# FNet mixing and top-1 expert layer on one core: row sums taken with the residual add, four one-hot tables on ScalarE, and the handover between the two stages re-ordered

## Chip, core and metric

One core of a Trainium2 chip runs the whole kernel. The metric is device time in microseconds (us); the number compared is the median of several runs. The engines are TensorE (PE; its weight loads are listed as PEld), VectorE (DVE), ScalarE (ACT), GpSimd (POOL) and SyncE (SP, which here only issues DMAs). Each runs its own instructions in order and waits for the others by semaphores.

## What is computed

The input is 2048 tokens of 512 values. The first half mixes them with a Fourier transform, the second sends each token to one of eight experts:

```python
x = A_x
h = x + Real(DFT_seq(DFT_hidden(layernorm(x))))      # by DFT matrices that are inputs
n = layernorm(h)
logits = n @ w_gate                                   # 8 experts
e = argmax(logits)                                    # top 1; its softmax over one value
out = h + gate * (silu(n @ w1[e]) @ w2[e])            # w1: 512 x 1376, w2: 1376 x 512
```

## The kernel before

**First half.** Tokens are folded by symmetry into 4 groups and 8 result blocks of 2 x 128 tokens; `second(i)` is the last product of block i (12 matmuls of 512 columns into one PSUM bank, `bank(i)`). `sums_of(i)` then adds the bank to the input rows (two row sets of 128 tokens: `direct` and `turned_row`, the latter as two instructions, 510 + 2 columns) and takes mean and variance of the two row sets. It has two ways: `far_stats`, two passes on ScalarE (a sum, then a square with that sum as bias, L247 and L248), for three of four row sets, and `own_stats` on VectorE (`bn_stats`, `bn_aggr`, L254 to L257) for the rest. `settle(c)` makes 1/deviation and -mean/deviation for four row sets (a square root on ScalarE, L264, six small VectorE instructions, L270 to L276) and stores the 512 values and these two numbers of each token to `rows` in DRAM (`leave`, L586, on SP). The last group (c = 3: row sets 12 to 15, "late") is not waited for in DRAM: its rows go straight from SBUF.

**Routing.** `gate(i)` makes the logits (small matmuls woven between those of `second`), `route` (L593 to L602, VectorE) picks the experts, `rank_them` (PE) and `take_ranks` (VectorE) number the tokens of each expert. `place(t)` writes a 128 x 304 one-hot table of row set t (`lanes == rank`, L640): t = 0 to 3 on GpSimd, the rest on VectorE. 16 matmuls (L849, "turned", into c2b) multiply them by `mine`, which holds token numbers and logits, so that each expert gets a list of its tokens. ScalarE copies the list (L850 `up`), PE turns it (L852), ScalarE copies it into `table` (L855).

**Handover.** Expert 0 comes first and takes up to 232 early tokens, gathered from `rows` by two indirect DMAs on GpSimd's queue (L865, into `hold`), plus up to 72 late ones. Ahead of the gathers stands a tiny read, `peek` (L857). The late ones: `spot(t)` (L647) makes 72-column one-hots for row sets 12 to 15, `normal_late` (L870) and L878 normalise these rows (`late`), and `late_rows` (L652) multiplies the two, 16 matmuls into c2a with a filler matmul behind each. `stand` (L887) turns the gathered rows (`xn`), `upright0` splits the turned rows into high and low parts (`t0h`, `t0l`). `split` is the helper for this everywhere: a cast on ScalarE (L117), a subtraction on VectorE (L118). `prep(b)` does the same to a weight block b ("pair"), `load(b)` fetches it. `fill(n)` issues n matmuls of ones by zeros, 512 columns, of which nobody uses the result (L376).

**Second half.** 8 experts x 11 steps (`first`: 12 matmuls into hp, silu twice on ScalarE, a subtraction on VectorE; `then`: 12 matmuls into yp). Beside it `recheck` compares the DFT matrices with the symmetries that the first half assumes (L700, VectorE, 32 pairs of 512 KB blocks and four more); `AT_ONCE` pairs are read and checked in the first half, one half pair per step in the second half.

**What sets the order.** PE, VectorE, ScalarE and SP run their instructions in the order in which the code stands; a line that stands later can't pass one that waits.

Of the kernel before, what the change touches and what calls it, by code (L numbers as in the profile page):

```python
# [8 lines left out]
F32 = mybir.dt.float32  # L9
# [31 lines left out]
AT_ONCE = 5  # L41
# [18 lines left out]
def fnet_moe(ctx: ExitStack, tc: tile.TileContext, xq, wrep, wline, wcol0, dmat, xturn, dturn, wcol, wchk, dchk, wsm, xres, wgen, dgen, wexp, out):  # L60
# [43 lines left out]
    peek = const.tile([NL, 8], F32, name="peek")  # L104
# [36 lines left out]

    def prep(b):
        if b in raws:
            ready[b] = halves()
            split(*ready[b], raws.pop(b))
# [15 lines left out]
    with ExitStack() as pa:  # L161
# [99 lines left out]
        def deviations(pool, n, mv):  # L261

            sd = pool.tile([P, n], F32, name=f"sd{n}")
            nc.scalar.activation(sd, mv[:, :, 1], AF.Sqrt, bias=eps)  # L264
            return sd

        def roots(pool, n, sd, mv, nm, to=None):
# [3 lines left out]
            nc.vector.tensor_scalar(v, mv[:, :, 1], EPS, -0.5, op0=ALU.add, op1=ALU.mult)  # L271
# [4 lines left out]
            nc.vector.scalar_tensor_tensor(nm_to, nm, 1.0 / ROOT, r_to, op0=ALU.mult, op1=ALU.mult)  # L276
# [210 lines left out]
        spots = stood.tile([P, NS - NL, LATE], F32, name="spots")  # L487
        ours = stood.tile([P, NS - NL], F32, name="ours")
# [79 lines left out]
        def direct(i):  # L568
            c, j = divmod(i, 2)
            x = X[c][:, 2 * j, :D]  # L570
            nc.vector.tensor_add(x, bank(i), x)
            return x

        def turned_row(i):
            c, j = divmod(i, 2)
            x, y = X[c][:, 2 * j + 1, :D], bank(i)
            two = x.rearrange("p (a c) -> p a c", a=2)
            nc.vector.tensor_add(two[:, :, 1:], ap(y, HALF + 1, [[-HALF, 2], [1, HALF - 1]]), two[:, :, 1:])
            nc.vector.tensor_add(x[:, 0::HALF], y[:, 0::HALF], x[:, 0::HALF])
            if i == 2 * SPEC:  # L580
                nc.scalar.copy(x[0:1, :], alone[0])
            return x
# [43 lines left out]
        def cards():  # L626

            nc.vector.tensor_sub(card[:, :, 1], tops, tops)
            for i in range(2):
                nc.vector.tensor_tensor(  # L630
                    mine[:, :, i, :], chosen, card[:, :, i:i + 1].bitcast(F32).to_broadcast([P, NS, E]), op=ALU.mult)

        def place(t, eng=None):
# [6 lines left out]
            (eng or nc.vector).tensor_scalar(places[t], lanes[:, :CAPS[0]], rank[:, t:t + 1], None, op0=ALU.is_equal)  # L640
# [3 lines left out]

        def spot(t):
            i = t - NL
            nc.vector.tensor_scalar(  # L647
                spots[:, i, :], lanes[:, EARLY:EARLY + LATE], rank[:, t:t + 1], ours[:, i:i + 1], op0=ALU.is_equal, op1=ALU.mult)
# [8 lines left out]
        w2 = {}  # L657
        gates = C[1][0][:, :TC].rearrange("p (i e) -> p i e", i=NS // 2)
        mvs, nms = {}, {}
        FAR_H = (0, 1, 2)  # L660
        POOLS = 4

        def sums_of(i):
# [4 lines left out]
            for q, fold in ((2 * j, direct), (2 * j + 1, turned_row)):  # L668
                x = {q: fold(i)}
                if q in FAR_H and (c, q) != (NCH - 1, 1):  # L670
                    far_stats(work, x, (q,), mvs[c], nms[c])
                else:
                    own_stats(work, x, (q,), mvs[c], nms[c])

        def settle(c, a=0, b=4):

            mv, nm = mvs[c][:, a:b, :], nms[c][:, a:b]
            roots(work, b - a, deviations(work, b - a, mv), mv, nm, (X[c][:, a:b, D], X[c][:, a:b, D + 1]))
            leave(c, a, b)
# [142 lines left out]
        check(2)  # L822
        load(0)
        load(1)
        load(2)
        run(second(3), several(gate(4), gate(5), gate(6), gate(7)), 4)
        lone_gate(*alone[1:])
        route()
        run(second(4))
        got = rank_them()  # L830
        sums_of(3)
        sums_of(4)
        run(second(5))
        take_ranks(*got)
        cards()
        for t in range(POOLS):
            place(t, nc.gpsimd)
        for t in range(POOLS, 10):
            place(t)
        sums_of(5)  # L840
        run(second(6))
        settle(1)
        settle(2)
        for t in range(10, NS):
            place(t)
# [8 lines left out]
        whole = table.rearrange("p q a e -> p (q a e)")  # L854
# [13 lines left out]
        def normal_late(t):  # L868
            x = X[3][:, t - NL, :]
            nc.scalar.activation(held[t], x[:, :D], AF.Identity, scale=x[:, D:D + 1], bias=x[:, D + 1:])  # L870

        sums_of(6)
        nc.vector.tensor_scalar(ours, whom[:, NL:], float(E), None, op0=ALU.is_equal)
        for t in range(NL, NS):
            spot(t)
        sums_of(7)
        settle(3)
        for t in range(NL, NS - 1):  # L878
            normal_late(t)
        x = X[3][:, 3, :]  # L880
        nc.vector.tensor_scalar(held[NS - 1], x[:, :D], x[:, D:D + 1], x[:, D + 1:], op0=ALU.mult, op1=ALU.add)
# [11 lines left out]
        for t in range(NL, NS):  # L893
            late_rows(upr[2], t)
        prep(0)
        prep(1)
        softmax(work, table[:, :, 1, :])
# [626 lines left out]
```

## Time and profile before

| | us |
|---|---|
| median of 3 runs | 434.7 (433.95 to 434.83) |
| the profiled execution | 432.62 |
| its span, first to last instruction | 430.9 |
| busy: PE, DVE, ACT, POOL | 403.3, 346.3, 251.0, 70.3 |

The profile is one execution. Its time lies 1.72 us above its span (launch and end) and 2.1 us below the median of the runs. Busy time says how much of the span an engine had work. A busy PE isn't PE at full rate: its clock has two levels here, 2.4 GHz (granted clock 1.00) and 1.2 GHz (0.50), and a matmul at the lower one shows up as busy for longer. The second half starts at 139.22 us, with the first matmul into hp.

### The profile page before, as it was taken

The numbers are of one execution on the slowest core, as the hardware profiler recorded it, in microseconds if no ns is written. First come the engines' busy times: TensorE is split into PE (matmuls) and PEld (weight loads), VectorE is DVE, ScalarE is ACT, GpSimd is POOL, SyncE is SP. The second block draws the span as 40 slices with busy tenths as digits, with TensorE's granted clock in tenths as the row PEclk, the third lists the DMA queues.
The fourth block names the chain that finished last, engine by engine and source line by source line (L and its number), as shares of the span: only waits on it lengthen the run. The fifth ranks groups of instructions, "written<-read, shape, count | busy, mean of one in ns | idle before, by whom it ended". The sixth has DMA issues, their size and how long they took to land. (4 is left out here: it accounts for less than half of the span.)

```text
span 430.9 us, 7840 instructions
## 1 busy us (share of the span) xinstructions
PE 403.3 (94%) x2769; PEld 358.7 (83%) x2769; DVE 346.3 (80%) x752; ACT 251.0 (58%) x482; POOL 70.3 (16%) x69
## 2 busy tenths in 40 slices
PE   5699999999778999999999999999999999899992
PEld 2489998878446999999999999998888888799981
DVE  3689975788964765698999899999999999866641
ACT  5989721614366565647556564665765665666640
POOL 1000000000320220332044023404304102300101
PEclk9699999999859999999999999999999999999998
DMA  8973453382166389669899989999999999754201
GB/s 295 412 270 120 175 199 115 137 288 94 68 213 205 108 310 363 202 232 376 326 322 370 343 300 346 378 358 355 366 348 376 400 372 386 232 192 163 86 0 53
DMA packets 32385, 110.43 MB, mean 256 GB/s; under 512 B 4113, under 2 KB 4113, under 8 KB 31698
## 3 DMA queue, kind: packets, MB, share of 16 engines
q1 hardware_dynamic: 29298, 100.77, 64.7%
q0 software_dynamic: 3040, 9.08, 5.9%
q8 instruction: 23, 0.38, 0.3%
q14 instruction: 24, 0.20, 0.1%
HBM read 101.44 MB, written 8.60 MB: 255 GB/s over the span
## 5 line engine op out<-in xcount | busy, mean ns | idle before, releaser
L117 ACT CAST pair<-far 128x1024 fp32r<-128x1024 f32 x77 | 80.7, 1049 | 55.3 <-PE yp L159 55.3
L118 DVE TENSOR_TENSOR pair<-far,pair 128x1024 fp32r<-128x1024 f32 x77 | 93.9, 1219 | 23.2 <-ACT pair L117 23.0
L157 PE MATMUL hp<-th,pair 128*128 128x256 f32 (+3 forms) x308 | 89.9, 292 | 2.4 <-DVE pair L118 2.4
L700 DVE CUSTOM_DVE_ANT_0 scrap<-raw 128x256 bf16<-128x256 f32 (+3 forms) x106 | 88.3, 833 | 1.9 <-DMA raw<-in_wchk 0.4
L158 PE MATMUL hp<-tl,pair 128*128 128x256 f32 (+3 forms) x308 | 87.6, 284 | 0.7 <-DVE tl L118 0.6
L159 PE MATMUL hp<-th,pair 128*128 128x256 f32 (+3 forms) x308 | 87.5, 284 | 0.0
L157 PEld LDWEIGHTS hp<-th,pair 128*128 128x128 f32 x308 | 58.0, 188 | 8.4 <-DVE pair L118 7.1
L992 ACT ACTIVATE sl<-hp 128x256 f32<-128x256 f32 (+4 forms) x88 | 34.5, 392 | 46.7 <-PE hp L159 45.1
L158 PEld LDWEIGHTS hp<-tl,pair 128*128 128x128 f32 x308 | 58.0, 188 | 2.3 <-DVE tl L118 1.3
L159 PEld LDWEIGHTS hp<-th,pair 128*128 128x128 f32 x308 | 58.0, 188 | 0.0
L157 PE MATMUL yp<-hh,pair 128*128 128x304 f32 (+3 forms) x176 | 53.0, 301 | 0.2 <-DVE yT L1024 0.2
L158 PE MATMUL yp<-hl,pair 128*128 128x304 f32 (+3 forms) x176 | 51.2, 291 | 0.0
L159 PE MATMUL yp<-hh,pair 128*128 128x304 f32 (+3 forms) x176 | 51.2, 291 | 0.0
L1040 POOL DMA_INDIRECT out_h<-o,ids x20 | 36.8, 1842 | 87.6 <-DVE o L1039 87.1
L996 DVE TENSOR_TENSOR hl<-sl,hh 128x256 fp32r<-128x256 f32 (+4 forms) x88 | 38.0, 432 | 6.2 <-ACT hh L995 3.5
L945 POOL DMA_INDIRECT hg<-rows,src x17 | 21.1, 1241 | 133.9 <-issue 49.2
L157 PE MATMUL yp<-pair,hl 128*128 128x512 f32 x88 | 35.6, 405 | 0.0
L158 PE MATMUL yp<-pair,hh 128*128 128x512 f32 x88 | 34.7, 395 | 0.0
L159 PE MATMUL yp<-pair,hh 128*128 128x512 f32 x88 | 34.6, 393 | 0.0
L995 ACT ACTIVATE hh<-hp 128x256 fp32r<-128x256 f32 (+4 forms) x88 | 34.1, 388 | 0.0
L157 PEld LDWEIGHTS yp<-hh,pair 128*128 128x128 f32 x176 | 33.1, 188 | 0.8 <-DVE yT L1024 0.4
L158 PEld LDWEIGHTS yp<-hl,pair 128*128 128x128 f32 x176 | 33.1, 188 | 0.0
(418 smaller groups left out, 803.8 us busy)
## 6 DMA issues: line engine op xcount, KB each, us to landing
far<-in_wexp SPq DMA_DIRECT2D x77, 512.0 KB, 7.2
raw<-in_wchk SPq DMA_DIRECT2D x64, 512.0 KB, 5.8
raw<-in_wexp SPq DMA_DIRECT2D x11, 512.0 KB, 5.4
rows<-x SPq DMA_DIRECT2D x4, 1028.0 KB, 6.1
raw<-in_wrep SPq DMA_DIRECT2D x8, 512.0 KB, 7.2
xt<-in_xturn SPq DMA_DIRECT2D x4, 1024.0 KB, 8.5
x<-in_xq SPq DMA_DIRECT2D x3, 1024.0 KB, 8.5
raw<-in_dchk SPq DMA_DIRECT2D x4, 512.0 KB, 5.3
```

Of the source, the lines that this page charges most:

```text
L117: nc.scalar.copy(hi, src)
L118: (eng or nc.vector).tensor_sub(lo, src, hi.bitcast(F32))
L157: nc.tensor.matmul(ps, sl, mh, start=first, stop=False)
L158: nc.tensor.matmul(ps, sh, ml, start=False, stop=False)
L159: nc.tensor.matmul(ps, sh, mh, start=False, stop=last)
L700: nc.vector.tensor_tensor_reduce(left, a, b, scale, 0.0, op, ALU.max, to)
L945: nc.gpsimd.indirect_dma_start(out=got[:n, i, :], out_offset=None, in_=rows, in_offset=bass.IndirectOffsetOnAxis(ap=src[:n, i:i + 1], axis=0))
L992: nc.scalar.activation(sl, ps, AF.Silu)
L995: nc.scalar.activation(hh, ps, AF.Silu)
L996: nc.vector.tensor_sub(hl, sl, hh.bitcast(F32))
L1040: d = nc.gpsimd.indirect_dma_start(out=out, out_offset=bass.IndirectOffsetOnAxis(ap=ids[:n, i:i + 1], axis=0), in_=o[:n], in_offset=None, ...
```

## The change

- `direct` and `turned_row` add by scalar_tensor_tensor with an accumulator, so that the sum over the row comes out of the add; for `turned_row` two partial sums are added by one more small instruction (L695 of the new code). ScalarE then takes one pass per row set (`spread`, a square with the sum as bias) instead of two, and `bn_stats`/`bn_aggr` are gone. One row set (of block 2, whose row 0 is replaced after the add) keeps a second ScalarE pass (`whole_sum`). `roots` and `deviations` take other constants for the other scale.
- `place`: row sets 4, 6, 8, 10 on ScalarE, each as two activations (Abs, then Relu of 1 - |x|); none on GpSimd. `cards` (which makes `mine`) goes from VectorE to GpSimd.
- `spot` and its tables are gone: `late_rows` uses columns 232 to 303 of the tables from `place`, and the factor that keeps only expert 0's tokens goes into the scale and bias of the late rows. One filler stands among the four products of a row set instead of four.
- Order: gates 6 and 7 run beside `second(4)` instead of `second(3)`, `sums_of(3)` ahead of `route`; `settle(1)` (and its store) ahead of `take_ranks`; `settle(2)` after three one-hots; the matmuls of "turned" run beside 8 fillers, and 22 fillers instead of 8 stand behind them, 6 instead of 3 ahead of hp, none around `stand`. The casts of the first two weight blocks (`high`) run ahead of `route`, four blocks are prepared ahead of hp instead of three. `peek` is gone. The exp of the gates, with its two table loads, goes into expert 0's second step; the rows of expert 1 are normalised after the silu of step 6 instead of before.
- `AT_ONCE` 4: one pair of `recheck` goes from the first half to the second.

VectorE, from the numbering of the tokens to the adds of the last group. Before (`x_123` is the third group's input, `fh`, `fl` are one-hot tables; some tables are GpSimd's and don't stand here):

```order
L624 SCALAR_TENSOR_TENSOR rank<-chosen,past,rank 128x4
L628 TENSOR_TENSOR card<-tops 128x16
L630 TENSOR_TENSOR mine<-chosen,card 128x16x8 x2
L640 TENSOR_SCALAR fh_1201<-lanes,rank 128x304 x2
L640 TENSOR_SCALAR fl_1204<-lanes,rank 128x304 x2
L640 TENSOR_SCALAR fh_1207<-lanes,rank 128x304 x2
L571 TENSOR_TENSOR x_123<-c0a,x_123 128x512
L578 TENSOR_TENSOR x_123<-c0a,x_123 128x2x255
L579 TENSOR_TENSOR x_123<-c0a,x_123 128x2
L254 BN_STATS st<-x_123 128x6
L255 BN_AGGR mv_1161<-st 128x2
L257 TENSOR_SCALAR nm_1162<-mv_1161 128x1
```

After (`x_124` is now the third group's input; the piece from the same instruction on):

```order
L633 SCALAR_TENSOR_TENSOR rank<-chosen,past,rank 128x4
L579 SCALAR_TENSOR_TENSOR x_124,nm_1195<-c3b,x_124 128x512
L586 SCALAR_TENSOR_TENSOR x_124,part<-c3b,x_124 128x2x255
L588 SCALAR_TENSOR_TENSOR x_124,part<-c3b,x_124 128x2
L695 TENSOR_TENSOR nm_1195<-part 128x1
L579 SCALAR_TENSOR_TENSOR x_124,nm_1195<-c0a,x_124 128x512
L586 SCALAR_TENSOR_TENSOR x_124,part<-c0a,x_124 128x2x255
L588 SCALAR_TENSOR_TENSOR x_124,part<-c0a,x_124 128x2
L695 TENSOR_TENSOR nm_1195<-part 128x1
L654 TENSOR_SCALAR fh_1214<-lanes,rank 128x304 x2
L654 TENSOR_SCALAR fl_1217<-lanes,rank 128x304
```

Both adds of the third group now stand ahead of every one-hot, each with its sum; the statistics on VectorE are gone.

ScalarE, from the table of tokens to the split of the turned rows. Before:

```order
L855 COPY table<-c1a 128x48
L247 ACTIVATE junk,nm_1313<-x_124 128x512
L248 ACTIVATE junk,mv_1312<-x_124,nm_1313 128x512
L247 ACTIVATE junk,nm_1313<-x_124 128x512
L248 ACTIVATE junk,mv_1312<-x_124,nm_1313 128x512
L264 ACTIVATE sd_1339<-mv_1312,eps 128x4
L870 ACTIVATE late<-x_124 128x512 x3
L117 CAST pair<-raw 128x1024 x2
L151 ACT_TABLE_LOAD
L151 ACTIVATE ex<-table 128x24
L899 ACT_TABLE_LOAD
L899 ACTIVATE warm<-eps 128x1
```

After:

```order
L891 COPY table<-c1a 128x48
L679 ACTIVATE junk,mv_1338<-x_125,nm_1339 128x512 x4
L273 ACTIVATE sd_1358<-mv_1338,eps 128x4
L905 ACT_TABLE_LOAD
L905 ACTIVATE warm<-eps 128x1
L919 ACTIVATE late<-x_125,ours 128x512 x3
L118 CAST t0h<-c2a 128x4x72
L118 CAST t0h<-c0a 128x4x128
L118 CAST t0h<-c3a 128x4x104
L145 CAST pair<-raw 128x1024 x2
```

The late group's statistics are still four passes, one per row set now; one table load stands ahead of `late`, and the casts of weights, the exp and the gathered rows' normalisation no longer stand between `late` and the split.

PE, the 16 matmuls that make the list of tokens ("turned", into c2b). Before (`fh_1195` and `fl_1198` are GpSimd's tables):

```order
L849 MATMUL c2b<-fh_1201,mine 16x304 x2
L849 MATMUL c2b<-fl_1204,mine 16x304 x2
L849 MATMUL c2b<-fh_1207,mine 16x304 x2
L849 MATMUL c2b<-fl_1256,mine 16x304 x2
L849 MATMUL c2b<-fh_1259,mine 16x304 x2
L849 MATMUL c2b<-fl_1262,mine 16x304 x2
L849 MATMUL c2b<-fh_1195,mine 16x304 x2
L849 MATMUL c2b<-fl_1198,mine 16x304 x2
L852 MATMUL c1a<-identr,up 128x16 x3
```

After, its last part (`fh_1244`, `fl_1249`, `fh_1254` and `fl_1259` are here the tables that ScalarE writes, row sets 4, 6, 8 and 10):

```order
L884 MATMUL c2b<-fh_1244,mine 16x304
L886 LDWEIGHTS ones
L886 MATMUL c2a<-zero,ones 128x512
L884 MATMUL c2b<-fl_1249,mine 16x304
L884 MATMUL c2b<-fh_1254,mine 16x304
L886 LDWEIGHTS ones
L886 MATMUL c2a<-zero,ones 128x512
L884 MATMUL c2b<-fl_1259,mine 16x304
L884 MATMUL c2b<-fh_1264,mine 16x304
L886 LDWEIGHTS ones
L886 MATMUL c2a<-zero,ones 128x512
L884 MATMUL c2b<-fl_1267,mine 16x304 x2
```

A filler now follows each second product, and GpSimd's four tables, last before, are replaced by ScalarE's, which stand three places from the end.

The diff, cut to its core:

```diff
-AT_ONCE = 5
+AT_ONCE = 4
...
-        def direct(i):
+        def direct(i, to):
...
-            nc.vector.tensor_add(x, bank(i), x)
+            nc.vector.scalar_tensor_tensor(x, bank(i), 1.0, x, op0=ALU.mult, op1=ALU.add, accum_out=to)
...
-        def place(t, eng=None):
+        def place(t, far=False):
...
-            (eng or nc.vector).tensor_scalar(places[t], lanes[:, :CAPS[0]], rank[:, t:t + 1], None, op0=ALU.is_equal)
+            if far:
+                gap = work.tile([P, CAPS[0]], F32, name="gap", bufs=2)
+                nc.scalar.activation(gap, lanes[:, :CAPS[0]], AF.Abs, scale=-1.0, bias=rank[:, t:t + 1])
+                nc.scalar.activation(places[t], gap, AF.Relu, scale=-1.0, bias=one)
+            else:
+                nc.vector.tensor_scalar(places[t], lanes[:, :CAPS[0]], rank[:, t:t + 1], None, op0=ALU.is_equal)
...
+        def spread(x, total, to):
+            junk = work.tile([P, D], BF16, name="junk", bufs=1)
+            nc.scalar.activation(junk, x, AF.Square, bias=total, scale=-float(D), accum_out=to)
...
+            x = direct(i, total[:, a:a + 1])
+            y = turned_row(i, part[:, 0:1], part[:, 1:2])
+            spread(x, total[:, a:a + 1], mv[:, a, 1:2])
+            if i == 2 * SPEC:
+                whole_sum(y, total[:, b:b + 1])
+            else:
+                nc.vector.tensor_add(total[:, b:b + 1], part[:, 0:1], part[:, 1:2])
+            spread(y, total[:, b:b + 1], mv[:, b, 1:2])
...
-        for t in (*range(POOLS, NS), *range(POOLS)):
-            nc.tensor.matmul(turned, flat(t), places[t], start=t == POOLS, stop=t == POOLS - 1)
+        order_t = [t for t in range(NS) if t not in FAR_T]
+        order_t[-3:-3] = FAR_T
+        for n, t in enumerate(order_t):
+            nc.tensor.matmul(turned, flat(t), places[t], start=n == 0, stop=n == NS - 1)
+            if n % 2:
+                nc.tensor.matmul(C[2][0], ones, zero, start=True, stop=True)
...
-                    spots[:, t - NL, :], start=t == NL and k == 0, stop=t == NS - 1 and k == KD - 1)
-                fill(1, 2, True)
+                    places[t].bitcast(F32)[:, EARLY:], start=t == NL + 1 and k == 0, stop=t == NS - 1 and k == KD - 1)
+                if k == 1:
+                    fill(1, 2, True)
...
-        fill(8, 2, True)
-        nc.gpsimd.dma_start(peek, rows.rearrange("(t p) d -> t p d", p=P)[:NL, 0, :8])
+        fill(FILL1, 2, True)
...
+                if (r, j) == (0, 1):
+                    softmax(work, table[:, :, 1, :])
+                    warm = work.tile([P, 1], F32, name="warm", bufs=1)
+                    nc.scalar.activation(warm, eps, AF.Silu)
```

## Rows read from the trace of the kernel before

**Rows 1.** Busy us by stretch: PE, PEld, DVE, ACT, POOL; clock, DMA share, GB/s.

```profile
117.00:121.00 4.00, 3.51 (x14) 1.79 (x14) 3.86 (x13) 0.45 (x2) 0.00 (x0) 0.50 1.03 366
...
300.00:350.00 50.00, 49.06 (x309) 42.25 (x309) 49.62 (x97) 31.99 (x61) 10.41 (x6) 1.00 1.00 374
```

**Rows 2.** PE's timeline, routing to second half: start, us, what, [idle before <-releaser].

```profile
100.65 0.16 PE L566 MATMUL c1a<-g,ah 1*1 1x8 f32 x1
...
112.72 0.44 PE L849 MATMUL c2b<-fh,mine 128*16 128x304 f32 x2
...
113.27 0.44 PE L849 MATMUL c2b<-fh,mine 128*16 128x304 f32 x2
116.73 0.72 PE L849 MATMUL c2b<-fl,mine 128*16 128x304 f32 x2 [3.02 <-DVE fl L640]
...
118.91 0.71 PE L849 MATMUL c2b<-fl,mine 128*16 128x304 f32 x2
...
120.84 3.59 PE L376 MATMUL c2b<-zero,ones 128*128 128x512 bf16 x8
126.45 0.70 PE L652 MATMUL c2a<-spots,late 128*128 128x72 f32 x2 [2.02 <-ACT late L870]
...
133.79 0.38 PE L376 MATMUL c2b<-zero,ones 128*128 128x512 bf16 x1
134.00 0.34 PE L652 MATMUL c2a<-spots,late 128*128 128x72 f32 x2
134.18 1.24 PE L376 MATMUL c2b<-zero,ones 128*128 128x512 bf16 x5
135.54 0.66 PE L887 MATMUL c0a<-ident,xn 128*128 128x128 f32 x4
136.03 1.03 PE L376 MATMUL c2b<-zero,ones 128*128 128x512 bf16 x4
...
139.22 1.38 PE L987 MATMUL hp<-t0h,pair 128*128 128x304 f32 x8
```

**Rows 3.** VectorE's timeline in the same stretch.

```profile
103.13 0.17 DVE L602 TENSOR_REDUCE early<-chosen 128x1 bf16<-128x12 bf16 x1
...
117.45 0.66 DVE L640 TENSOR_SCALAR fl<-lanes,rank 128x304 fp32r<-128x304 f32 x2
118.03 0.68 DVE L571 TENSOR_TENSOR x<-c0b,x 128x512 f32<-128x512 f32 x1
...
124.58 0.18 DVE L270 RECIPROCAL r<-sd 128x4 f32<-128x4 f32 x1 [0.56 <-ACT sd L264]
```

**Rows 4.** ScalarE's timeline in the same stretch.

```profile
121.80 0.72 ACT L248 ACTIVATE junk<-x,nm 128x512 bf16<-128x512 f32 x1
...
122.65 0.63 ACT L247 ACTIVATE junk<-x 128x512 bf16<-128x512 f32 x1
...
125.59 2.22 ACT L870 ACTIVATE late<-x 128x512 f32<-128x512 f32 x3 [1.04 <-DVE x L276]
...
129.71 1.28 ACT L151 ACT_TABLE_LOAD   x1
131.01 0.22 ACT L151 ACTIVATE ex<-table 128x24 f32<-128x24 f32 x1
```

**Rows 5.** The page's group of the check's passes.

```profile
L700 DVE CUSTOM_DVE_ANT_0 scrap<-raw 128x256 bf16<-128x256 f32 (+3 forms) x106 | 88.3, 833 | 1.9 <-DMA raw<-in_wchk 0.4
```

**Rows 6.** Line L700, its accumulator reads: ns min/median/max, first and last start.

```profile
L700 DVE DVE_READ_ACCUMULATOR2_ANT off<- x108: 70/82/88, 72.0 to 371.5; 128x1 f32 x108
```

**Rows 7.** VectorE's timeline in the second half: an add by scalar_tensor_tensor.

```profile
299.85 0.74 DVE L1039 SCALAR_TENSOR_TENSOR o<-tp,usel,hg 128x512 f32<-128x512 f32 x1
```

**Rows 8.** Waits from 300 to 380 us: total, times, longest.

```profile
PEld hp L157 <- DVE pair L118: 6.5, 14, 1.3
```

**Rows 9.** DMA issues: KB each, median us from issue to landing.

```profile
rows<-x SPq DMA_DIRECT2D x4, 1028.0 KB, 6.1
...
hold<-rows,src POOLq DMA_INDIRECT x5, 4.4
```

More of the change, by code (lines that the diff above doesn't have):

```diff
@@ L140, in halves, with high, low @@
         return both[:, 0, :], both[:, 1, :]
+    def high(b):
+        ready[b] = halves()
+        nc.scalar.copy(ready[b][0], raws[b])
+    def low(b):
+        hi, lo = ready[b]
+        nc.vector.tensor_sub(lo, raws.pop(b), hi.bitcast(F32))
     def prep(b):
         if b in raws:
-            ready[b] = halves()
-            split(*ready[b], raws.pop(b))
+            high(b)
+            low(b)
     def softmax(pool, z):
@@ L667, in sums_of, with settle @@
                 mvs[c], nms[c] = fresh_stats(work, 4)
[L668 to L678, printed above, removed]
+            mv, total = mvs[c], nms[c]
+            part = work.tile([P, 2], F32, name="part")
+            a, b = 2 * j, 2 * j + 1
+            x = direct(i, total[:, a:a + 1])
[6 more added lines that the diff above has]
+            spread(y, total[:, b:b + 1], mv[:, b, 1:2])
+        def settle(c, a=0, b=4, between=None):
+            mv, total = mvs[c][:, a:b, :], nms[c][:, a:b]
+            unit = float(D) ** -3
+            sd = deviations(work, b - a, mv, unit)
+            if between:
+                between()
+            roots(work, b - a, sd, mv, total, (X[c][:, a:b, D], X[c][:, a:b, D + 1]), unit, -1.0 / D)
             leave(c, a, b)
@@ L821, in fnet_moe @@
         sums_of(2)
[L822 to L826, printed above, removed]
+        for b in range(4):
+            load(b)
+        run(second(3), several(gate(4), gate(5)), 2)
+        sums_of(3)
+        fourth = second(4)
+        last_gates = several(gate(6), gate(7))
+        for _ in range(2):
+            next(fourth)
+            for _ in range(KD):
+                next(last_gates)
         lone_gate(*alone[1:])
+        high(0)
+        high(1)
         route()
-        run(second(4))
+        run(fourth)
         got = rank_them()
-        sums_of(3)
+        settle(1)
+        cards()
+        take_ranks(*got)
+        run(second(5))
         sums_of(4)
[L833 to L838, printed above, removed]
+        sums_of(5)
+        for t in range(3):
             place(t)
-        sums_of(5)
+        settle(2)
         run(second(6))
[L842 to L845, printed above, removed]
+        mixed = [(t, t in FAR_T) for t in range(3, NS)]
+        for t, far in mixed:
+            place(t, far)
         run(second(7))
         turned, standing = C[2][1][:2 * E, :CAPS[0]], C[1][0]
-        for t in (*range(POOLS, NS), *range(POOLS)):
-            nc.tensor.matmul(turned, flat(t), places[t], start=t == POOLS, stop=t == POOLS - 1)
+        whole = table.rearrange("p q a e -> p (q a e)")
+        order_t = [t for t in range(NS) if t not in FAR_T]
[4 more added lines that the diff above has]
+                nc.tensor.matmul(C[2][0], ones, zero, start=True, stop=True)
         nc.scalar.copy(upright[:, :CAPS[0]], turned)
@@ L891, in upright0 @@
             split(T0[0][:, :, lo:lo + n], T0[1][:, :, lo:lo + n], ps)
-        for t in range(NL, NS):
+        for t in (NL + 1, NL, *range(NL + 2, NS)):
             late_rows(upr[2], t)
-        prep(0)
-        prep(1)
-        softmax(work, table[:, :, 1, :])
-        warm = work.tile([P, 1], F32, name="warm", bufs=1)
-        nc.scalar.activation(warm, eps, AF.Silu)
-        upright0(2, EARLY, LATE)
+        low(0)
         with nc.allow_low_precision(reason="counts up to 18"):
@@ L911, in fnet_moe @@
             x = xg0[:n, i, :]
-            if i:
-                nc.vector.tensor_scalar(xn0[:n, i, :], x[:, :D], x[:, D:D + 1], x[:, D + 1:], op0=ALU.mult, op1=ALU.add)
-            else:
-                nc.scalar.activation(xn0[:n, i, :], x[:, :D], AF.Identity, scale=x[:, D:D + 1], bias=x[:, D + 1:])
-            fill(4, 2, True)
-            stand(i)
+            nc.vector.tensor_scalar(xn0[:n, i, :], x[:, :D], x[:, D:D + 1], x[:, D + 1:], op0=ALU.mult, op1=ALU.add)
+        stand(0)
+        stand(1)
+        upright0(2, EARLY, LATE)
+        for i, n in front:
             upright0(i, i * P, n)
+        low(1)
         prep(2)
-        fill(3, 2, True)
+        load(6)
+        prep(3)
+        fill(6, 2, True)
     with ExitStack() as pb:
```

75 lines of the change are left out of this document (37 added, 38 removed).

## The prediction, as it went on record

> **What bounds the kernel now.** I read busy time by stretch first. From 139 us on PE is busy nearly throughout, so whatever moves the first hp matmul (139.22 [rows 2]) moves the end, as long as the second half keeps its length. Ahead of it PE's timeline names two waits: 3.02 us for VectorE's one-hots, up to 116.73, and 2.02 us for ScalarE's late rows [rows 2]. Behind the first the granted clock is 0.50, its lower level, in 117 to 121 [rows 1]. What comes behind runs at the lower clock: eight fillers take 3.59 us [rows 2], 0.45 each, against 0.21 later (133.79 to 134.00 [rows 2]); the 16 late products with their fillers take 126.45 to 134.18 [rows 2], 7.7 us. From there to hp are another 5.0 us. So the stretch from 113 to 139 is a chain VectorE, PE, ScalarE, VectorE, ScalarE, PE, in which each engine waits for one other, and half of it is PE at half clock.
>
> **The list of tokens.** The last gate matmul ends at 100.81, VectorE's route at 103.30 [rows 2, 3], 2.5 us behind it; PE fills this with `second(4)` and doesn't wait. Now half of that block (6 matmuls of 512 columns, at the filler's 0.21 [rows 2] 1.3 us) stands ahead of the last gates: route starts 1.3 us later, half a block is left to cover its 2.5 us, and PE waits about 1.1. So the numbering, and all of PE behind it, come 1.0 us later; the first product of "turned" starts at 113.7 instead of 112.72 [rows 2]. These take 0.14 each at the full clock (two pairs in 0.55, 112.72 to 113.27 [rows 2]), 16 of them 2.2, and the eight new fillers 1.7: the end is at 117.6 if PE never waits, against 119.62 now (118.91 and 0.71 [rows 2]).
>
> Does VectorE keep up? No row shows an add that gives its sum. The plain add takes 0.68 [rows 3], scalar_tensor_tensor on the same shape 0.74 [rows 7], an accumulator read 0.08 [rows 6]; nearest to it is 0.74 and 0.08, of which some 0.08 overlaps with the next instruction (two adds start 0.60 apart for 0.68 long ones). I take 0.75, with 0.66 (the read is free) and 1.48 (twice the plain 0.74) as ends. With the two-column add, its read and the sum of the parts a call of `sums_of` is then 1.95 us, no shorter than now on average: it saves ScalarE's passes, not VectorE's time. Behind route (104.6 now) VectorE has: `settle` 1.0 (124.58 to 125.59, where ScalarE's `late` gets its rows [rows 3, 4]), the ranks 1.3, two `sums_of` 3.9, three one-hots at 0.29 (two in 0.58, 117.45 to 118.03 [rows 3]) 0.9, `settle` 1.0, nine one-hots 2.6, with 0.4 of waits 115.7. PE wants the last at 117.3: 1.6 us of cover. ScalarE's four tables are eight passes of 304 columns, at most half of a 512-column pass (0.72 [rows 4]) plus a fixed part, 2.5 to 3 us from 112: done by 115, wanted at 116.5. The order shows no table load among them. GpSimd's `mine` has from 104.6 to 113.7. PE waits no more in this step, so the clock stays up.
>
> **Late group.** The way from the list's end to the fillers (1.2 us, 119.62 to 120.84 [rows 2]) has three small matmuls at full clock now, 0.3 less: ScalarE is free 2.2 earlier. It has four passes before the root, as before, but all of the longer kind: 0.85 from start to start (121.80 to 122.65 [rows 4]) against 0.76, +0.2. So `settle(3)` starts 2.0 earlier, at 122.6, and ends at 123.6. VectorE has its last sums at 119.6 (115.7 and 3.9) and the fourth pass starts at 121.4: cover 1.8. Then: the factors 0.2, row set 13 on VectorE 0.7, first late product 124.5. ScalarE's table load starts at 122.6, takes 1.28 [rows 4], hides behind `settle`'s small instructions and is over at 124.1 with its dummy; three late rows at 0.74 (2.22 for three [rows 4]) are ready at 124.8, 125.6, 126.3. A row set on PE is four products at 0.18 (134.00 to 134.18 [rows 2]) and one filler, 0.93: end at 128.2, against 134.18. The 22 fillers (4.6 us from 118.6) end at 123.2, so PE waits 1.3 us in front.
>
> The Trainium skill (ScalarE: Activation LUTs, What ACT_TABLE_LOAD costs) gives 2.66 us for a switch of tables, drain included; here the next activation starts 1.30 after the load [rows 4]. By the page three late rows would come 1.3 later, and hp with them.
>
> **To hp.** Gathered rows: the third group's store is issued at 113.1, with the median 6.1 us [rows 9] down at 119.2, about when the list is there; the gathers land 4.4 later [rows 9], at 123.7 and 125.1. Without `peek` nothing else stands ahead of them. VectorE wants them at 126.4 (behind `low(0)` 1.15 and the counts 0.75) and is done at 127.6, before PE is free. Then eight transposes (four in 0.49, 135.54 to 136.03 [rows 2]) 1.0, and six fillers 1.3, behind which the last cast (0.5) hides: hp at 130.5, against 139.22. **Gain 8.7 us.** If the gathers landed later, each us behind 126.4 would cost one.
>
> **Second half.** (a) One more pair of the check: 88.3 us [rows 5] for 34 pairs (32, and the four blocks counted as two) is 2.6 us of VectorE. From 300 to 350 it is busy for 49.62 of 50 [rows 1], and PE's weight loads wait for its pairs 14 times, 6.5 us up to 380 [rows 8]: there VectorE sets the pace. But each step has one half pair anyway; the added one lengthens the check by two steps at its end, into steps where VectorE has room. Between 0 and 2.6 I take 1.2. (b) Two table loads and the exp in expert 0's second step, 3.0 us of ScalarE. Four blocks lie ready instead of three and the step after needs no new one; ends 0 and 3.0, I take 0.3, since silu is wanted only two steps later. (c) Loads: the fifth block waits for `low(1)` and is issued 1 us behind hp; it has some 10 us. Nothing.
>
> **Sum:** -8.7 + 1.2 + 0.3 = -7.2. On the profiled execution 432.6 gives 425.4; it ran 2.1 below the median, so 434.7 gives **427.5**.
>
> **Rivals.**
> 1. *The clock falls all the same*, in the 1.3 us ahead of the late rows. Against it: before, it fell behind a wait of 3.02, more than twice as long. For it: the margins above add up, a chain 1.5 us longer makes that wait twice as long. Price: 16 products and four fillers at half clock, 3.7 more. 431.2.
> 2. *The second half gives it back*: the whole 2.6 for the pair and 3.0 for the loads, 4.1 more than taken. For it: VectorE's 49.62 of 50. 431.6.
> 3. *Half rate for the adds.* Two inputs and an accumulator might need two cycles an element: 0.60 more for each long add, 1.2 a call. One-hots 2.4 later, beyond their cover by 0.8; four calls make the last sums 4.8 later, beyond theirs by 3.0; the wait ahead of the late rows passes 3 us and rival 1 comes on top: 6.7, 434.2. Against it: the check's passes read two inputs and accumulate, and a 1024-column one takes about twice a 512-column add. The Trainium skill (Vector Engine (DVE) Microarchitecture Reference, Points that are easy to get wrong) says that scalar_tensor_tensor with two SBUF sources that aren't bf16 runs at half throughput, since no port is left for the accumulator. One source here is PSUM, so the sentence may not apply; no run here shows it.
> 4. *Slower than before*: the same add costs 1.48 and its read, 0.82 more. The calls grow by 1.64, the last sums come 6.6 later, 4.8 beyond their cover, with the clock 8.5: 436.0. It decides from 0.7 us more per add, where 3.5 of chain and 3.7 of clock eat up 7.2.
>
> **Chances.** Forecast 0.62 (its own range 425 to 429.5), rival 1 0.17, rival 2 0.11, rival 3 0.05, rival 4 0.05. About 0.9 us, 0.2%, can be told from no change: faster 0.90, same 0.05 (rival 3), slower 0.05 (rival 4). For 8 in 10 the range needs the forecast and the first two: 424.5 to 432.
>
> **What will show it.** In the new profile: the granted clock stays 1.00 from 104 to hp (else rival 1); the turned products run without a wait and end near 117.6; the last `spread` is followed by `settle(3)` near 122.6; hp near 130.5; an add with its sum lasts 0.74 with a read of 0.08 behind it (1.2 or more: rivals 3, 4); from hp to the end it is some 1.5 us longer than before (over 4: rival 2). Wrong would be: a wait of PE for tables of ScalarE, for `mine` or for gathered rows, of which I find none.

## The result, and the profile after

The kernel after takes 423.81 us (median of 4 runs, 423.56 to 425.54), the kernel before 434.76 (4 runs): ratio 0.9755, 95% interval 0.9722 to 0.9789. Run again in a later comparison it took 423.25 (6 runs, 422.87 to 425.4), ratio 0.9775 (0.9743 to 0.9808). The direction was forecast; the forecast of 427.5 was 3.7 too high, and the time lies 0.7 below the range.

| profiled execution | before | after |
|---|---|---|
| time, span | 432.62, 430.9 | 423.7, 421.9 |
| first hp matmul | 139.22 | 130.05 |
| from there to the end of the span | 291.7 | 291.9 |
| busy: PE, DVE, ACT, POOL | 403.3, 346.3, 251.0, 70.3 | 400.1, 339.5, 252.6, 66.6 |

All of the 9 us lie ahead of hp. PE's timeline of after, where [rows 2] showed waits of 3.02 and 2.02 us (start, us, what, [idle before <-releaser]):

```profile
103.92 0.22 PE L617 MATMUL c2a<-chosen,before 128*128 128x128 bf16 x1 [0.73 <-DVE chosen L609]
...
113.01 0.44 PE L884 MATMUL c2b<-fh,mine 128*16 128x304 f32 x2
113.29 0.39 PE L886 MATMUL c2a<-zero,ones 128*128 128x512 bf16 x1
...
116.85 0.39 PE L886 MATMUL c2a<-zero,ones 128*128 128x512 bf16 x1
117.50 0.50 PE L889 MATMUL c1a<-identr,up 16*128 16x16 f32 x3 [0.26 <-ACT up L887]
117.93 4.92 PE L385 MATMUL c2b<-zero,ones 128*128 128x512 bf16 x22
123.66 0.67 PE L661 MATMUL c2a<-fh,late 128*128 128x72 f32 x4 [0.81 <-DVE late L917]
...
127.56 0.56 PE L661 MATMUL c2a<-fl,late 128*128 128x72 f32 x4
127.95 0.60 PE L925 MATMUL c0a<-ident,xn 128*128 128x128 f32 x4
...
130.05 1.36 PE L1018 MATMUL hp<-t0h,pair 128*128 128x304 f32 x8
```

The list's products run without a wait, the late products take 4.3 us instead of 7.7, and hp follows the transposes by 2 us. The clock no longer falls in 117 to 121, where [rows 1] had 0.50, and VectorE is as full in 300 to 350 as it was (columns as in [rows 1]):

```profile
117.00:121.00 4.00, 3.74 (x20) 1.83 (x19) 0.39 (x5) 3.27 (x9) 1.64 (x3) 1.00 0.00 0
300.00:350.00 50.00, 48.95 (x312) 42.88 (x311) 49.55 (x104) 31.10 (x59) 6.24 (x4) 1.00 0.99 366
```

VectorE's timeline of after, the adds that give their sums, against the plain add of [rows 3]:

```profile
106.33 0.68 DVE L579 SCALAR_TENSOR_TENSOR x<-c3b,x 128x512 f32<-128x512 f32 x1
106.94 0.08 DVE L579 DVE_READ_ACCUMULATOR x<-c3b,x 128x1 f32 x1
106.94 0.68 DVE L586 SCALAR_TENSOR_TENSOR x<-c3b,x 128x510 f32<-128x510 f32 x1
...
107.75 0.16 DVE L695 TENSOR_TENSOR nm<-part 128x1 f32<-128x1 f32 x1
107.83 0.69 DVE L579 SCALAR_TENSOR_TENSOR x<-c0a,x 128x512 f32<-128x512 f32 x1
...
121.84 0.18 DVE L279 RECIPROCAL r<-sd 128x4 f32<-128x4 f32 x1 [4.42 <-ACT sd L273]
...
125.34 1.00 DVE L941 TENSOR_SCALAR xn<-hold 128x512 f32<-128x512 f32 x2
```

The next add starts 0.61 after the one before: the read lies under it, and the sum costs nothing. A call of `sums_of` takes 1.50 us (106.33 to 107.83). The gathered rows (`hold`) are there when VectorE wants them: no wait stands at 125.34.

### The profile page after: what moved, and what is told of

Read it like the earlier page. It is cut to its first block, busy times and chain, and to the rows that moved or that the text cites. A ratio compares the mean times of both kernels' runs of the same rounds, so it can differ in the third digit from the quotient of the medians.

```text
span 421.9 us, 7857 instructions
## 1 busy us (share of the span) xinstructions
PE 400.1 (95%) x2774; PEld 356.1 (84%) x2774; DVE 339.5 (80%) x763; ACT 252.6 (60%) x481; POOL 66.6 (16%) x67
```

## The experiments

Executions of one kernel differ by 3 us and more, so a time says little here about half a microsecond. One distance in the profile says more: from VectorE's first instruction of `route` to the first hp matmul, called the **path** below. It is 28.39 to 28.42 us in the profiles of after, e1, e4, e15 and e16. It is 38.37 us before (100.85 to 139.22) and 28.42 after (101.63 to 130.05); of the 9.95 us between them 3.6 lie ahead of the first late product, 3.4 in the late products, 2.9 behind them. Where the clock fell behind the gates (last section) the path is longer, by 0.62 in e11, the one profile of the kernel after with that fall; such kernels are set against its 29.04. "Rest" is hp to the end of the span, good to 0.1. Each kernel is the kernel after with one edit, where nothing else is said.

| kernel | median us | ratio to before | path | rest |
|---|---|---|---|---|
| after | 423.81 | 0.9755 | 28.42 | 291.9 |
| e11_again | 423.25 | 0.9775 | 29.04, clock fell | 292.2 |
| e1_pair_back | 424.43 | 0.9777 | 28.41 | 293.1 |
| e2_sums_back | 424.39 | 0.9789 | 28.49 | 292.4 |
| e3_no_fill | 427.89 | 0.9853 | 31.68 | 292.3 |
| e4_dve_hots | 425.64 | 0.9826 | 28.40 | 292.2 |
| e5_slow_add | 425.60 | 0.9805 | 30.26, clock fell | 291.5 |
| e6_spread_early | 424.28 | 0.9774 | 27.47, clock fell | 292.2 |
| e7_before_filled | 430.60 | 0.9934 | 36.47 | 292.6 |
| e8_before_sums | 432.43 | 0.9970 | 38.18 | 291.7 |
| e9_exp_back | 422.84 | 0.9759 | 29.16, clock fell | 291.3 |
| e10_late_fill | 426.25 | 0.9854 | 30.44 | 292.3 |
| e12_short | 422.35 | 0.9761 | 27.03 | 291.9 |
| e13_gates_back | 424.24 | 0.9786 | 30.01 | 292.7 |
| e14_shorter | 422.62 | 0.9753 | 26.77 | 290.8 |
| e15_gate_fill | 425.78 | 0.9820 | 28.40 | 294.0 |
| e16_peek_back | 425.50 | 0.9805 | 28.39 | 294.3 |
| e17_old_order | 430.25 | 0.9937 | 33.27, clock fell | 292.5 |
| e18_casts_back | 425.23 | 0.9827 | 29.35 | 293.0 |

**The sums, undone in the new kernel and put alone into the old one.** e2 has the old `direct`, `turned_row`, `sums_of` and `settle` (the functions printed above) with the new order. e8 is the kernel before with the new ones:

```diff
-            nc.vector.tensor_add(x, bank(i), x)
+            nc.vector.scalar_tensor_tensor(x, bank(i), 1.0, x, op0=ALU.mult, op1=ALU.add, accum_out=to)
```

> The changed kernel with the old sums: plain adds, two passes on ScalarE for three of four row sets, bn_stats on VectorE for the rest; the order and the fillers stay. Theory (the order and the fillers carry most of the gain): VectorE gets about 1 us more ahead of its last one-hots and some 2.5 more up to the last sums, ScalarE two passes more ahead of its four tables, which come 1.4 us later; PE waits up to 1 us in the list's products, hp 0.6 to 1.5 later, clock up, time 424.4 to 425.5. Rival (the add with the sum carries most of it): chain 3 us longer, the wait ahead of the late rows passes 3 us, the clock falls, 428 or more.

> The kernel before with the add that gives its sum and one ScalarE pass per row set, and nothing else of the change. Theory (by itself it shortens VectorE's way to the last one-hot by about 1.2 us and little else): PE's wait 1.8 instead of 3.02, list 1.2 earlier, hp 1 to 1.5 earlier, 1 to 1.5 below the median of before. Rival 1 (the shorter wait keeps the clock up): 3 or more below. Rival 2 (ScalarE's long passes take the place of the short ones, nothing comes earlier): within 0.5.

Undone, the path is 0.07 longer, not the 0.6 to 1.5 expected; alone, it is 0.19 shorter, not 1 to 1.5: PE's wait for the tables falls from 3.02 to only 2.48, and the clock falls as before. The time of e8 is below before (0.9949 to 0.9992), more than its path explains; that remainder stays open. For hp the sums by themselves bring next to nothing, in either kernel.

**The tables.** e4: `FAR_T = ()`, all 16 on VectorE.

> The changed kernel with all 16 one-hot tables on VectorE, none on ScalarE. VectorE gets four more at 0.29, 1.2 us: last table 115.5, wanted by PE at 116.4, last sums at 118.5, wanted by ScalarE's third late pass at 119.8. Theory (cover everywhere): hp as far behind route as before the edit (28.4 us within 0.2), time 423.5 to 424.5. Rival (ScalarE's share of the tables is needed, since the chain runs through VectorE): hp 0.9 to 1.2 later, 424.8 to 425.5.

The path is unchanged: cover everywhere, as the theory says. The median lies above the expected 424.5 with a profile at 423.9; nothing in the path accounts for that. The other three executions ran at a mean clock of 0.982 to 0.984, the profile at 0.987.

No run puts tables back on GpSimd, `cards` back on VectorE, or `spot` back. So what removed PE's wait of 3.02 is only in part shown (e13 below brings some of it back). The rows of before point at the first two. While GpSimd wrote its tables (108.1 to 112.4), VectorE took 1.16 us for two one-hots, and 0.66 later:

```profile
110.23 2.17 POOL L640 TENSOR_SCALAR fl<-lanes,rank 128x304 fp32r<-128x304 f32 x2
110.89 1.16 DVE L640 TENSOR_SCALAR fh<-lanes,rank 128x304 fp32r<-128x304 f32 x2
...
116.88 0.66 DVE L640 TENSOR_SCALAR fh<-lanes,rank 128x304 fp32r<-128x304 f32 x2
```

The six one-hots of that stretch took 3.07 us (108.90 to 111.97), the six behind it 1.73, and `cards` took 0.76 ahead of them. That is 2.1 us of VectorE ahead of the last table which the kernel after doesn't have. That GpSimd's tables are what slowed VectorE is not tested.

**Slower adds.** e5 reads the bank twice more in each call:

```diff
+            for _ in range(2):
+                nc.vector.scalar_tensor_tensor(scrap[:, :D], bank(i), 1.0, x, op0=ALU.mult, op1=ALU.add, accum_out=part[:, 2:3])
```

> The changed kernel with two more passes of 512 columns by scalar_tensor_tensor with a sum (results not used) in each call of sums_of, 1.2 us per call, four calls behind the numbering: what adds at half rate would have cost. Theory: last sums at 122.2 instead of 117.3, 1.5 us later than the last late pass starts now; one-hots done at 116.8, PE waits 0.5 for them; hp about 2 us later, the wait ahead of the late rows 2.5 to 3 us, clock up: 425.5 to 426.5. Rival, the price of the prediction's rival 3 (beyond 3 us the clock falls): 6.7 above its forecast's step, here 429 to 431.

The path grows by 1.2 (30.26 against 29.04), less than the 2 expected: the 4.8 us on VectorE (a call takes 2.71 us instead of 1.50) are mostly covered. The wait ahead of the late rows is 1.20 instead of 0.81, not 2.5 to 3, since the list comes later too and the fillers with it. So 1.2 us more per call don't cost the prediction's 6.7. Its calls at half rate would have been 3.15 us long (1.95 and 1.2), longer than e5's; that length was not run.

**The fillers and the clock.** e3 takes the eight out of the list's products and leaves 8 of 22 behind it; e10 puts 16 back among the late products; e7 is the kernel before with 14 fillers after the table of row set 9 and `fill(26, 2, True)` for `fill(8, 2, True)`.

```diff
-            if n % 2:
-                nc.tensor.matmul(C[2][0], ones, zero, start=True, stop=True)
...
-        FILL1 = 22
+        FILL1 = 8
```

> The changed kernel without the eight fillers among the list's products and with 8 fillers behind them instead of 22. Theory (the fillers only keep the clock up, rival 1 of the prediction prices it at 3.7 us for the late rows): the list is done 1.4 to 1.8 us earlier and ScalarE's late passes with it, PE waits over 3 us ahead of the late rows, the granted clock falls there to 0.50, late products take twice as long: hp 1 to 3 later than 130.05, 425 to 427. Rival (the clock isn't what the fillers buy): hp 1.4 earlier, 422.4.

> The changed kernel with 16 fillers among the late products again instead of 4. Theory (PE alone sets the pace there): 12 fillers at 0.22, hp 2.6 later than 28.4 behind route, 426.2 to 426.8. Rival (ScalarE's late rows or the gathered rows set it): hp less than 1.5 later.

> The kernel before with nothing changed but fillers: 14 in the 3.02 us in which PE waits for VectorE's tables, and 26 instead of 8 behind the list, so that the clock stays up. Theory (the clock is about a third of the gain): list done 1.4 earlier, late products twice as fast up to 130 us, but ScalarE's and VectorE's chain to the gathered rows only 1.4 earlier: hp 1.5 to 3 earlier, 1.5 to 3 below the median of before in this batch. Rival (the clock is half of the gain or more): 4.4 or more below.

PE's timeline of e3:

```profile
117.16 1.90 PE L385 MATMUL c2b<-zero,ones 128*128 128x512 bf16 x8
122.89 1.13 PE L661 MATMUL c2a<-fh,late 128*128 128x72 f32 x4 [3.82 <-DVE late L915]
```

Two stretches of e3 (columns as in [rows 1]):

```profile
125.00:129.00 4.00, 4.00 (x19) 3.82 (x19) 0.56 (x2) 0.00 (x0) 0.00 (x0) 0.50 0.61 206
129.00:133.00 4.00, 4.00 (x21) 3.74 (x21) 0.63 (x2) 1.08 (x3) 0.00 (x0) 0.52 0.00 0
```

The list is ready 1.3 us earlier, PE waits 3.82, and behind that wait the clock is 0.50: the late products and their fillers take 8.2 us instead of 4.3. Net the path is 3.26 longer. In e10 it is 2.02 longer for 12 fillers, 0.17 each (2.6 and 0.22 expected): PE sets the pace there. In the kernel before, fillers alone keep the clock at 1.00 and bring 1.90 of path and 0.3% to 1.0% of time.

**The order on VectorE, and the stores behind it.** e17:

```diff
-        settle(1)
-        cards()
-        take_ranks(*got)
-        run(second(5))
         sums_of(4)
+        run(second(5))
+        take_ranks(*got)
+        cards()
+        for t in range(10):
+            place(t, t in FAR_T)
         sums_of(5)
...
+        settle(1)
+        settle(2)
+        for t in range(10, NS):
+            place(t, t in FAR_T)
```

> The changed kernel with VectorE's order between the numbering and the list as it was: sums_of(4) ahead of take_ranks, ten tables, sums_of(5), settle(1) and settle(2), the last six tables. Sums, ScalarE's tables, fillers stay. Theory (since neither the sums nor ScalarE's tables alone carry it, the order does): settle(1) and settle(2) wait for ScalarE, whose passes stand behind its tables, the last tables are 1 us or more late for PE, the third group's rows are stored 2 us later and the gathers wait for them: hp 1 to 3 later than 28.4 behind route, 425 to 427. Rival (the parts cover for each other: with the cheaper sums the old order fits too): hp within 0.5, 423.5 to 424.5.

The list is not later: ScalarE's copy of it starts 16.04 behind route, as in e11. The path is 4.2 us longer all the same. The store of the third group, as its line's view gives it (duration in ns, start, who waited for it, time to landing), and then the timelines of GpSimd, VectorE and PE, all of e17:

```profile
L595 SPq DMA_DIRECT2D rows<-x x1: 395/395/395, 114.8 to 114.8; - x1
...
  POOL hold L899: 3.4, 1
...
DMA to landing us min/median/max: 7.9/7.9/7.9
```

```profile
120.14 0.23 POOL L896 TENSOR_SCALAR src<-table 128x2 int32<-128x2 f32 x1 [14.21 <-ACT table L890]
123.81 1.19 POOL L899 DMA_INDIRECT hold<-rows,src  x1 [3.44 <-issue]
...
128.73 0.55 DVE L940 TENSOR_SCALAR xn<-hold 128x512 f32<-128x512 f32 x1 [1.48 <-DMA hold<-rows,src]
132.87 0.55 DVE L940 TENSOR_SCALAR xn<-hold 104x512 f32<-104x512 f32 x1 [3.59 <-DMA hold<-rows,src]
133.47 0.64 PE L924 MATMUL c3a<-ident,xn 104*128 104x104 f32 x4 [3.09 <-DVE xn L940]
```

Two stores leave together at 114.0 and 114.8, the second lands at 122.7, and the gathers wait for it, VectorE for the gathers, PE for VectorE. Of the 4.2 us, 3.3 lie ahead of these last transposes and about 1 behind the wait, where the granted clock is 0.61 (133 to 137). In the kernel before the stores were as late: they left at 115.6 and 116.4, its tiny read waited 2.35 us of issue, its gathers left at 124.95. In the kernel after the stores leave at 105.2 and 111.9 and land 4.6 and 4.7 us later; the gathers leave as soon as the list is there:

```profile
L595 SPq DMA_DIRECT2D rows<-x x1: 394/394/394, 111.9 to 111.9; - x1
...
DMA to landing us min/median/max: 4.7/4.7/4.7
```

```profile
118.32 0.23 POOL L897 TENSOR_SCALAR src<-table 128x2 int32<-128x2 f32 x1 [13.59 <-ACT table L891]
119.28 1.19 POOL L900 DMA_INDIRECT hold<-rows,src  x1 [0.73 <-POOL src L897]
```

Undone by itself, this order costs more than any other part: the earlier `settle(1)` and `settle(2)` matter by way of their stores. (e17 moves both with the tables and the numbering; no run moves one store alone.) The theory had the stores right; of its late tables nothing was seen. It doesn't follow that the order made 4.2 us of the gain. In the kernel before, the gathered rows landed at 131.5 and 134.3 and no engine waited for them. ScalarE and VectorE read them later, with the late products running until 134.2:

```profile
134.67 0.81 ACT L915 ACTIVATE xn<-hold 128x512 f32<-128x512 f32 x1
...
137.46 0.54 DVE L913 TENSOR_SCALAR xn<-hold 104x512 f32<-104x512 f32 x1
```

In the kernel after, VectorE wants them at 125.34. The early stores let what the other parts gained reach hp.

**The rest of the handover.** e18 casts the first two weight blocks behind the late products (`high(0)`, `high(1)` ahead of `low(0)` instead of ahead of `route()`); e16 puts `peek` back ahead of the gathers; e13 puts gates 6 and 7 beside `second(3)` and `sums_of(3)` behind `rank_them`; e9 moves the exp and both table loads from step 1 to the line ahead of `stand(0)`.

> The changed kernel with the casts of the first two weight blocks behind the late products again instead of ahead of route. Theory: ScalarE has the 2.0 us free there, but VectorE's subtraction of the first block stands ahead of the gathered rows and now waits for the cast, to 126.5: rows of the gather normalised 2 us later, at 128.7, transposes too: hp 1.5 to 2.5 later than 28.4 behind route, 425.5 to 426.3. Rival (only ScalarE's time counts, and it has some): hp within 0.3.

> The changed kernel with the tiny read of the stored rows ahead of the gathers on GpSimd's queue again. Theory (the gathered rows have 1.6 us of cover in front of the transposes, the read takes about 1 us of the queue): hp as far behind route as without it, 28.4 within 0.2, time equal within 0.4. Rival (the read's landing is waited for): gathers 1 to 2 us later, xn waits, hp up to 1 us later.

> The changed kernel with gates 6 and 7 beside second(3) again, as before, and sums_of(3) behind the numbering's matmuls as before. Theory: route starts 0.8 to 1.3 earlier, PE needs a whole second(4) ahead of the numbering and no longer waits 0.73 for it, so the list's products start 0.3 earlier; the 1.5 us of sums_of(3) on VectorE lie in its cover; hp 0.3 to 0.5 earlier, time 0.3 to 0.5 below the changed kernel. Second question: in 101 to 107 us the granted clock stays 1.00 if the denser gates are what drops it, and falls now and then if they aren't. Rival: the later one-hots make PE wait, 0.5 to 1 above.

> The changed kernel with the exp of the gates and its two table loads ahead of the turned rows again, behind the gathered rows on both engines. Theory (a load is 1.3 us and ScalarE waits 2.7 us for PE there anyway): hp 0.2 to 0.6 later behind route than the 28.4 of the changed kernel, the second half 0.3 shorter (its first three steps lose 0.27 to the loads now), time equal within 0.4. Rival: by the Trainium skill (ScalarE: Activation LUTs, What ACT_TABLE_LOAD costs) two loads are 5.3 us and reach 2.6 beyond the wait, hp 2.5 later, 426.2.

e18: 0.93 longer, on the path expected but half the size. e16: nothing on the path, as expected; its time is 1.7 us and more above after's, where 0.4 was allowed, with two waits for DMAs in the second half (1.8 and 1.6 us), and whether the read has to do with them isn't settled. e13: route 0.8 earlier but path 1.6 longer, hp 0.8 later than after: the rival. Of the 1.6, 0.5 lies ahead of the list's first product; the rest lies in the products, where PE waits for one-hots (0.53 us for the first it waits for). e9: path 0.12 longer than e11's, and the steps of the second half run 0.5 ahead of the kernel after's. By these profiles, moving the exp into the second half cost 0.4 us; the medians (422.84 and 423.25) lie too close to tell. ScalarE's timeline of e9:

```profile
126.73 1.28 ACT L160 ACT_TABLE_LOAD   x1
128.02 0.22 ACT L160 ACTIVATE ex<-table 128x24 f32<-128x24 f32 x1
128.26 1.28 ACT L905 ACT_TABLE_LOAD   x1
129.56 0.20 ACT L905 ACTIVATE warm<-eps 128x1 f32<-128x1 f32 x1
```

A load is 1.28 us, the next activation starts 1.29 after it.

**The pair of the check.** e1: `AT_ONCE = 5` and `check(2)` behind `sums_of(2)`.

> The changed kernel with AT_ONCE 5 and the pair of the check put back behind sums_of(2), where it stood before. Theory (the extra pair costs the second half nothing, since it only lengthens the check into steps where VectorE has room): from the first hp matmul to the end the span stays at 291.8 us within 0.3; VectorE's idle time ahead of route (1.97 and 2.38 us in the changed kernel) takes the 2.6 us, hp at 130.0 to 130.5, time 423.6 to 424.4. Rival, term (a) of the prediction: the second half gets 1.2 shorter (up to 2.6), time 421.5 to 422.8.

The check ends 5 us earlier (last accumulator read at 363.1 instead of 368.2), but no expert's eleven steps are shorter by more than 0.06 us: from expert 1's first step to expert 3's last it takes 107.28 us with the pair back and 107.27 without. The rest is 1.2 us longer, where the theory allowed 0.3; 0.8 of it is a wait for gathered rows in expert 0, the remainder is smaller delays that aren't told apart. So the pair costs the second half nothing that shows.

**Spread, and what limits next.** e15 puts four fillers among the small matmuls of gates 6 and 7. e6, e12 and e14 write `sums_of(6)` ahead of the copy of the list, with 14, 17 and 14 fillers behind the list; e12 and e14 take the fillers from the late products, put 3 between the transposes and 4 and 3 ahead of hp; e12 also drops those among the list's products, e14 moves the exp as e9.

> The changed kernel once more, as it is, in five rounds. Theory (the clock sometimes falls for 3 to 4 us behind the last gates, as in the profiles of e5 and e6 and not in that of the changed kernel, and this makes the spread): executions with a mean clock of 0.986 to 0.988 take 423.4 to 424.2, those with 0.981 to 0.984 take 1.5 to 2 us more, median 423.8 to 425. Rival: the times don't go with the clock.

> The changed kernel with four fillers of 512 columns among the small matmuls of gates 6 and 7. Theory (these small matmuls are what drops the clock behind them in some executions): no execution below a mean clock of 0.986, all within 1 us of each other, 0.9 above the fast ones of the changed kernel: 424.0 to 424.6. Rival (the fall comes from something else): some executions at 0.981 to 0.985 and 1.5 to 2 us longer, as before the edit.

> The changed kernel with sums_of(6) written ahead of ScalarE's copy of the list, so that two of the four late passes fill the 2.1 us in which ScalarE waits for the list, and 14 fillers instead of 22. Theory (the late group's chain through ScalarE sets hp): roots 1.7 us earlier, late products too, gathered rows just in time; hp 1.5 to 1.7 earlier, 422.1 to 422.6. Rival (gathered rows or the list set it): gain under 0.8, 423.2 or more.

> The changed kernel with two of the late passes ahead of ScalarE's copy of the list, no fillers among the list's products and the late products, 17 fillers instead of 22 behind the list, 3 between the two groups of transposes and 4 instead of 6 ahead of hp. Theory: list ready for ScalarE 1.0 to 1.3 earlier but taken up behind the two passes (0.3 earlier), roots 1.9 earlier, late products 2.5 us long instead of 4.3, gathered rows wanted as they land: hp 2.5 to 3.2 earlier than 28.4 behind route, 421 to 421.5. Rival 1 (gathered rows land late and PE waits for them, the clock falls): hp less than 1.5 earlier. Rival 2 (without the fillers the clock falls ahead of the late rows): 424 or more.

> The changed kernel with two late passes ahead of the copy of the list, the eight fillers among the list's products kept, 14 fillers behind the list, none among the late products, 3 between the transposes, 3 ahead of hp, and the exp with its table loads ahead of hp again. Theory: as in e12 the gathered rows set the transposes, but the clock stays 1.00 from 113 us on, so late products take 2.6 instead of 3.6 us and end before the gathered rows are there; hp 2 to 2.4 earlier than 28.4 behind route, second half 0.4 shorter by the exp: 420.8 to 421.8. Rival (gathered rows come later with the list): 422.3 or more.

e11's six executions: mean clock 0.987 or 0.988 with 422.87 to 423.28 (four) and 424.51, 0.984 with 425.4: the time mostly goes with the clock, not always. In e15 all six are at 0.985 or above, but they spread over 2.6 us and their median missed the expected 424.0 to 424.6: the clock isn't all of it. Its profile shows the other part, a wait of 2.06 us on ScalarE for expert 1's gathered rows:

```profile
154.16 1.52 ACT L985 ACTIVATE xg<-hg 128x512 f32<-128x512 f32 x2 [2.06 <-DMA hg<-rows,src]
```

The path of e6 is 1.57 shorter than e11's, as expected, but its time, 424.28, missed the expected 422.1 to 422.6 and isn't below after's. In e12 the clock is 0.60 in 117 to 121, and it still gains 1.4 of path, not 2.5 to 3.2: VectorE waits 1.10 us for the gathered rows, its rival 1. e14 keeps the clock and gains 1.65, less than the 2 to 2.4 expected; there too VectorE waits for the gathered rows:

```profile
125.52 0.55 DVE L939 TENSOR_SCALAR xn<-hold 104x512 f32<-104x512 f32 x1 [1.23 <-DMA hold<-rows,src]
```

e12 has a ratio of 0.9761 (0.9725 to 0.9796) beside 0.9775 of the kernel after in the same comparison, e14 one of 0.9753 in another: shorter paths, but a gain in time of 0.1% to 0.2% that these runs don't establish.

## Why the prediction was right and wrong, point by point

- **What bounds it, and rival 1's price: right.** hp moved, the second half kept its length. In e3 the late products pay 3.9 us at the lower clock; rival 1 said 3.7.
- **List of tokens: nearly.** PE waits 0.73 (1.1 said), the first product starts at 113.01 (113.7), ScalarE takes the list at 117.05 (117.6). ScalarE's tables take 4.2 us (110.76 to 114.94), not 2.5 to 3: a pass of 304 columns is 0.53 to 0.55, where the working took at most half of 0.72 and a fixed part; they are still in time.
- **The add with its sum: mis-sized.** 0.75 was taken, 0.61 from start to start measured; the low bound, 0.66, was nearer. A call is 1.50 instead of 1.95, the last one-hot is written 1.3 earlier than forecast, the last sums 2.3 earlier. It moved hp by little, since ScalarE's copy of the list stands ahead of the late passes. Rivals 3 and 4 fall with it. The page rule on half throughput (the Trainium skill, Vector Engine (DVE) Microarchitecture Reference, Points that are easy to get wrong) speaks of two SBUF sources; with one in PSUM the rows show the plain add's 0.68.
- **Late group and the way to hp: right in mechanism, 0.45 too long.** Roots 121.84 (122.6), late products 123.66 to 127.95 (124.5 to 128.2), hp 130.05 (130.5). Gain 9.17 against 8.7. The gathered rows were called a condition, with the store at 113.1; e17 shows that 4.2 us hang on this condition, the most of any part that was undone. The 2.66 us of the Trainium skill (ScalarE: Activation LUTs, What ACT_TABLE_LOAD costs) isn't what e9 shows: 1.29 from the start of a load to the next activation.
- **Second half: wrong.** Forecast +1.5, measured +0.2 (291.7 to 291.9). Term (a), 1.2 for the pair, is nothing that e1 shows; it was taken from the middle of a range though the text itself had the reason for its low end. Term (b), 0.3, is 0.4 to 0.5 (e9).
- **From the profile to the median: wrong, and the largest miss.** By its own sum the profiled execution was to be 425.4 and is 423.7: 1.7, of which 1.3 second half and 0.45 handover. The other 2.0 are the 2.1 added for the distance of one profile to a median of three runs. In the later comparisons the median of before is 433.3 to 434.1, 0.7 to 1.5 above its profile; after's profile lies 0.1 below its own, and in e11, the same kernel, the profile lies 2.15 above its median. This distance belongs to single executions, not to the kernel.

## What to carry to other kernels

Undo each part by itself, and read the distance between two events of the path where whole runs differ by 3 us and more. But don't take what a part costs when undone for its share of the gain. Here e17, e3, e10, e13 and e18 cost 4.2, 3.3, 2.0, 1.6 and 0.9 us of path, 12.0 together, for a gain of 9.95: a chain over several engines lets one part through only when the others are in place. Ask of every read from DRAM which store it waits for and where that store is issued: here two small blocks of VectorE work, moved ahead, let the stores leave early, and without that PE waits 3.09 us for the gathered rows. Don't carry a profile's distance from its median over to another kernel without executions of both.

## What the runs showed of the hardware

- The sum that a scalar_tensor_tensor gives costs nothing beside a plain add when one source is PSUM: 0.68 us for 512 columns, the read of 0.08 under the next instruction.
- Four kernels ran at the lower clock behind a wait of PE of 2.5 to 3.8 us (before, e3, e8, e17); waits of 0.7 to 1.2 us behind matmuls of 512 columns left it at 1.00 (after, e5). In e12 it fell behind the list's products without fillers and a wait of 1.46.
- It also falls with no idle time of PE in front. In 5 of 15 profiles with gates 6 and 7 packed as in the kernel after (e5, e6, e9, e11, e17) it is 0.50 to 0.53 in 103 to 105 us, behind the gates' matmuls of 8 to 32 columns; in the four profiles with gates as before (before, e7, e8, e13) and in e15 it is 1.00. Those are too few to call the packing the cause. Two kernels of the same code, after and e11:

```profile
103.00:105.00 2.00, 1.27 (x20) 1.13 (x20) 1.79 (x10) 0.00 (x0) 0.78 (x2) 1.00 0.00 0
```

```profile
103.00:105.00 2.00, 2.00 (x9) 1.30 (x8) 1.80 (x8) 0.20 (x1) 0.63 (x2) 0.50 0.00 0
```

- Two stores that leave together land late: after 5.1 and 7.9 us at 114.0 and 114.8 (e17), after 4.6 and 4.7 for the same stores 6.7 us apart (after).
